# A planner that prices transfers beside weight loads differently, with its order searched anew, in an attention and MoE kernel

## The chip, the cores and the metric

The kernel runs on one NeuronCore of a Trainium2 chip. The metric is the device time of one execution in microseconds (us); lower is better. One launch computes everything.

## The reference, cut to what matters

```python
q, k, v: (4, 8, 768, 64)   proj: (64, 6)   moe_w_in: (512, 2048)   moe_w_out: (2048, 512)

q_bucket = bits of (q @ proj > 0) as one number; k_bucket the same
scores = where(q_bucket[:, None] == k_bucket[None, :], q @ k.T / 8, -1e9)
attn = exp(scores - max); attn = attn / (sum + 1e-9)
x = attn @ v                      # heads side by side: (3072, 512)
h = x @ w_in; g = s * max(h, 0)**2 + b
out = g @ w_out                   # (3072, 512)
```

All of it is in 32-bit floating point.

## The kernel before, in words

**Work.** There are 32 visits, one for each batch and head, and each has three slots of 256 queries, 96 slots in all. A slot's scores go into three banks of PSUM: six leading matmuls (L656 or L658), then a maximum over the keys on VectorE (L664), its transposes on TensorE (L675, L679) with reductions on VectorE (L677, L686), six more matmuls that add the negative maximum (L696 or L698), three exponentials on ScalarE (L703), and the products with the values (L726, later L728 and L729). The first 27 slots (9 visits) use plain float32 in their value products; the rest split each operand into two parts. For some visits the queries are split in the same way: they are loaded, transposed and split (L476 and L490 on TensorE or L493 on VectorE, then L498, L499), hashed (L514 or L527 to L532, with L540, L543, L544 behind them), and parts are copied between tiles by several DMAs that SyncE (SP) issues (L225). From the ninth visit on, q and k come in four small loads (L442) and are transposed on VectorE (L493).

**MoE.** When the eight heads of a batch have a chunk of 256 tokens ready, it goes through a DRAM tile (xd, then xc) and the two MoE matrix products follow (L814, L831). They are TensorE work that may stand anywhere between the slots' steps. None can start before the first batch's heads are done, that is before 24 slots.

**Weights.** They arrive as 32 loads of 512 KB that ScalarE (ACT) issues (L391, tile `raw`, 128 rows of 4 KB), each unpacked by two ACT instructions (L392, L393), two on VectorE (L394, L395), and more on GpSimd and ACT (L396, L398, L404). Two of them may be under way before they are unpacked (`PACE = 2`).

**Values.** From the tenth visit on, a visit's values come through one tile `vn` (L598), which ACT casts into `vs` (L603), VectorE sums (L601) and GpSimd splits (L604). ACT works strictly in its order, so what stands behind L603 waits with it; so do VectorE and SP.

**What sets the order.** All steps are added to a `Plan` with an engine, an assumed cost, a priority and, for DMAs, an assumed service time (`lag`). `Plan.order` plays a list schedule through and gives each engine one fixed order. The priority of a step is moved by `NUDGE`, a table of numbers by code line and part of the run. The plan's times are only for sorting: on the chip an instruction starts when its semaphores allow it. Two rules of the plan matter here. One assumes that TensorE slows to half speed for 3.4 us when a running figure `warm`, which falls with gaps, is under a threshold. The other is the service of DMAs; before, all shared one counter:

```python
            if lag:
                moved = max(moved, start + cost) + lag
                end = moved + LAND
```

PSUM bank 4 is shared by the small transposes, the hash matmuls (L514, L527 to L532), the sums (L578, L614) and the transposes of queries (L476, L490), one group at a time. So such a matmul right behind an L679 can't start before VectorE's L686 has read the bank.

Of the kernel before, what the change touches and what calls it, by code (L numbers as in the profile page):

```python
# [31 lines left out]
class Plan:  # L32
# [41 lines left out]
    def order(self):  # L74
# [13 lines left out]
        moved = held = late = 0.0  # L88
# [21 lines left out]
        while len(out) < n:  # L110
# [20 lines left out]
            elif e == POOL:  # L131
                cost += max(0.0, held - start)
            elif e == PE:
                part = 1 / (1 + (start - free.get(PE, 0.0)) / 6)
                warm *= part * part
                if warm < 0.48:
                    late = start + 3.4
                if start < late:
                    cost *= 2
                part = 1 / (1 + cost / 6)  # L140
                warm = 1 - (1 - warm) * (part * part)
            free[e] = start + cost
            end = start + cost + HOP[e]
            if lag:
                moved = max(moved, start + cost) + lag
                end = moved + LAND
            out.append((start, i))
# [28 lines left out]
LAND = 1.3  # L176
# [11 lines left out]
def lsh_attention_moe(ctx: ExitStack, tc, q, k, v, proj, w_in, w_out, s, b, out):  # L188
# [181 lines left out]
    def decode(u, pr):  # L370
# [20 lines left out]
        plan.add(ACT, 0.33, lambda: nc.scalar.dma_start(raw(), src.rearrange("p (n t) -> p n t", t=2)), KK("a") if u < PACE else [], rk + [("pace", u % PACE)], pr - 5, 2.2)  # L391
# [644 lines left out]
```

## Time and profile before

| | before |
|---|---|
| median of 3 runs | 985.3 us (982.86 to 987.53) |
| the profiled execution's own time | 986.14 us |
| its span, first to last instruction | 984.4 us |
| TensorE busy (PE) | 958.5 us, 97% |
| VectorE (DVE), ScalarE (ACT), GpSimd (POOL) busy | 705.9, 703.9, 681.2 us |
| mean granted TensorE clock | 0.997 |

PE is matmuls on TensorE, PEld its weight loads. Of the profiled execution's time 1.7 us lie around the span. A busy share is over the whole span: the attention of the first 24 slots, the mixed stretch and the MoE tail have different limits, so the stretches are read apart.

### The profile page before, as it was taken

The page shows a single profiled execution, that of the slowest core. Times are in us where ns is not written, and L with a number is a line of the kernel's source. Part 1 is how long each engine was busy: PE and PEld are TensorE (multiplying, and loading weights), DVE is VectorE, ACT ScalarE, POOL GpSimd, SP SyncE. Part 2 cuts the span into 40 slices and gives each one's busy share as a digit, 9 for nine tenths or more (in the row PEclk, how much of TensorE's full clock was granted, in tenths as well). Part 3 has the DMA queues.
Part 4 walks back from the last instruction along what each step waited for, and adds up shares of the span by engine and source line. Part 5 has one row for each costly group of instructions (what it writes and reads, how often), then busy time and mean ns, then how long its engine had stood idle before and what let it go on. Part 6 is the DMA issues. An engine that isn't in the chain of part 4 may idle for free.

```text
span 984.4 us, 17823 instructions
## 1 busy us (share of the span) xinstructions
PE 958.5 (97%) x6322; PEld 865.4 (88%) x6322; DVE 705.9 (72%) x1081; ACT 703.9 (72%) x1365; POOL 681.2 (69%) x641
## 2 busy tenths in 40 slices
PE   8989988999999999999999999999999999999998
PEld 7877766789999999999899999999899999989997
DVE  6897776988988898888888898888888876100000
ACT  4777766888788887879788878878787877433332
POOL 3686756779787787879697887879687878522222
PEclk9999999999999999999999999999999999999999
DMA  6583766533433443342533433442523310201000
GB/s 172 163 225 107 211 167 144 151 77 72 121 89 82 101 103 69 111 105 61 138 72 89 115 89 70 115 103 63 143 57 91 108 45 2 96 21 45 33 22 22
DMA packets 133680, 95.21 MB, mean 97 GB/s; under 512 B 101464, under 2 KB 106328, under 8 KB 133592
## 3 DMA queue, kind: packets, MB, share of 16 engines
q1 hardware_dynamic: 128248, 77.03, 31.0%
q10 hardware_dynamic: 5344, 17.05, 5.9%
q8 instruction: 50, 0.82, 0.4%
q14 instruction: 38, 0.31, 0.1%
HBM read 50.40 MB, written 18.87 MB: 70 GB/s over the span
## 4 chain that ended last, share of the span: by engine, by line
PE 88%; DVE 4%; DMA 3%; ACT 2%; issue 1%; POOL 1%; SPq 0%; DVEq 0%; ACTq 0%; POOLq 0%
PE bank L814 27%; PE bank L831 26%; PE bank L658 6%; PE bank L726 6%; PE bank L698 5%; PE bank L729 5%; PE bank L728 5%; PE bank L656 2%; DMA xc<-xd 1%; PE bank L679 1%; DVE mx L664 1%; PE bank L761 1%; PE bank L527 1%; PE bank L528 1%; DVE osb L395 1%
## 5 line engine op out<-in xcount | busy, mean ns | idle before, releaser
L814 PE MATMUL bank<-xc,w 128*128 128x256 f32 x2304 | 346.6, 284 | 2.5 <-DMA xc<-xd 2.3
L722 POOL TENSOR_TENSOR hl<-et,hl 128x512 fp32r<-128x512 f32 x207 | 267.3, 1321 | 83.6 <-ACT hl L721 78.8
L814 PEld LDWEIGHTS bank<-xc,w 128*128 128x128 f32 x2304 | 309.3, 190 | 10.5 <-DMA xc<-xd 2.8
L831 PE MATMUL bank<-w,ghb 128*128 128x512 f32 x768 | 251.7, 396 | 0.0
L822 POOL TENSOR_TENSOR glb<-rb,ghb 128x512 fp32r<-128x512 f32 x96 | 124.8, 1300 | 106.7 <-ACT ghb L821 103.8
L664 DVE TENSOR_REDUCE mx<-bank 128x256 f32<-128x1536 f32 x96 | 168.3, 1753 | 9.6 <-ACT nat L540 2.9
L703 ACT ACTIVATE et<-bank 128x512 f32<-128x512 f32 x234 | 129.1, 626 | 45.0 <-PE bank L698 30.8
L748 DVE TENSOR_REDUCE zb<-et 128x256 f32<-128x1536 f32 x69 | 120.9, 1752 | 52.3 <-ACT et L703 52.1
L831 PEld LDWEIGHTS bank<-w,ghb 128*128 128x128 f32 x768 | 136.2, 188 | 19.1
L831 PE MATMUL bank<-w,glb 128*128 128x512 f32 x384 | 152.2, 397 | 0.0
L721 ACT CAST hl<-et 128x512 fp32r<-128x512 f32 x207 | 125.4, 672 | 0.0
L819 ACT ACTIVATE rb<-bank 128x512 f32<-128x512 f32 x96 | 57.2, 596 | 93.0 <-PE bank L814 91.8
L658 PE MATMUL bank<-aq,ks 84*128 84x256 f32 x504 | 108.1, 301 | 0.2 <-ACT ex L703 0.2
L728 PE MATMUL bank<-hl,vs 128*128 128x256 f32 x414 | 107.3, 283 | 0.0
L729 PE MATMUL bank<-hl,vs 128*128 128x256 f32 x414 | 107.0, 282 | 0.0
L768 ACT ACTIVATE xpb<-bank,vmn 64x256 f32<-64x256 f32 x96 | 45.1, 470 | 66.5 <-PE bank L729 42.9
L658 PEld LDWEIGHTS bank<-aq,ks 84*128 84x128 f32 x504 | 80.1, 190 | 5.4 <-ACT ex L703 0.4
L729 PEld LDWEIGHTS bank<-hl,vs 128*128 128x128 f32 x414 | 78.5, 190 | 6.6 <-POOL hl L722 0.2
L728 PEld LDWEIGHTS bank<-hl,vs 128*128 128x128 f32 x414 | 78.0, 188 | 6.7 <-issue 0.2
L831 PEld LDWEIGHTS bank<-w,glb 128*128 128x128 f32 x384 | 72.2, 188 | 12.4 <-POOL glb L822 0.2
L839 DVE SCALAR_TENSOR_TENSOR osb<-bank,misc,bcs 128x512 f32<-128x512 f32 x22 | 16.3, 747 | 89.0 <-PE bank L831 88.7
L698 PE MATMUL bank<-bq,ks 128*128 128x256 f32 x504 | 79.4, 288 | 0.0
(144 smaller groups left out, 1581.7 us busy)
## 6 DMA issues: line engine op xcount, KB each, us to landing
xd<-xsb SPq DMA_DIRECT2D x48, 256.0 KB
xc<-xd SPq DMA_DIRECT2D x48, 256.0 KB
raw<-in_moe_w_in_dram ACTq DMA_DIRECT2D x16, 512.0 KB
raw<-in_moe_w_out_dram ACTq DMA_DIRECT2D x16, 512.0 KB
vn<-in_v_dram SPq DMA_DIRECT2D x34, 192.0 KB
out_dram<-osb SPq DMA_DIRECT2D x22, 256.0 KB
ks<-aq SPq DMA_DIRECT2D x28, 192.0 KB
ks<-bq SPq DMA_DIRECT2D x28, 192.0 KB
```

Source lines behind the costliest of these rows:

```text
L658: nc.tensor.matmul(o, ks[0:HR + NR, 0, kt], aq[0:HR + NR, cs], start=m == 0, stop=m == 1, skip_group_check=True)
L664: dve(S * TPC, lambda: nc.vector.tensor_reduce(t, sc, AX.XY, ALU.max), [("b", b) for b in pb], [tk], pr, 1.75)
L698: nc.tensor.matmul(o, ks[:, 1, kt], bq[:, cs], start=False, stop=m == 1, skip_group_check=True)
L703: act(512, lambda p=p, z=z: nc.scalar.activation(et(z) if plain(i) else pairs(z), bank[:, pb[p]] if plain(i) else bank[:, pb[p]].rearrange ...
L721: act(512, lambda z=z, y=y: nc.scalar.copy(HL[2 * y].rearrange("p (m n) -> p m n", n=CH), pairs(z)), [("e", z)], [("hl", 2 * y)], pr, 0.05)
L722: pool(512, lambda z=z, y=y: nc.gpsimd.tensor_tensor(HL[2 * y + 1].rearrange("p (m n) -> p m n", n=CH), pairs(z), f32(HL[2 * y]).rearrange ...
L728: nc.tensor.matmul(av, VS[x][:, kt], HL[2 * y][:, ms], start=(kt == 0), stop=False)
L729: nc.tensor.matmul(av, VS[x][:, kt], HL[2 * y + 1][:, ms], start=False, stop=(kt == NT - 1))
L748: dve(S * TPC, lambda: nc.vector.tensor_reduce(ZB, es, AX.XY, ALU.add), [("e", z) for z in range(NE)], ["zb"], pr, 1.75)
L814: nc.tensor.matmul(hp, wt[("wi", n, cc)][:, m % 2, fs], xc[:, m // 2, :], start=(cc == 0 and m == 0), stop=(cc == NC_ - 1 and m == 2))
L822: pool(2 * CH, lambda r=r, gh=gh, gl=gl: nc.gpsimd.tensor_tensor(gl, r, f32(gh), ALU.subtract), [rk, hk], [lk], MP)
L831: nc.tensor.matmul(bank[:, 6 + t, :], (gh, gh, gl)[n][:, ts], wt[("wo", f)][:, n % 2], start=(f == 0 and n == 0), stop=(f == NF - 1 and n ...
```

## The change: what it does

Three things change in the planner, and none in what is computed. The threshold of `warm` rises from 0.48 to 0.54. Transfers get two counters: one for SP, on which a transfer takes up to twice its service while a weight load is still being served, and one for ACT's weight loads, which SP's transfers don't delay; a weight load's assumed service rises from 2.2 to 3.0 us. And the table `NUDGE` has new numbers throughout. The loads themselves stay as they were: rows of 4 KB.

```diff
-        moved = held = late = 0.0
+        moved = loads = held = late = 0.0
...
-                if warm < 0.48:
+                if warm < 0.54:
                     late = start + 3.4
...
-            if lag:
-                moved = max(moved, start + cost) + lag
+            if lag and e == SP:
+                moved = max(moved, start + cost)
+                moved += lag + min(lag, max(0.0, loads - moved))
                 end = moved + LAND
+            elif lag:
+                loads = max(loads, start + cost) + lag
+                end = loads + LAND
...
 -        plan.add(ACT, 0.33, lambda: nc.scalar.dma_start(raw(), src.rearrange("p (n t) -> p n t", t=2)), KK("a") if u < PACE else [], rk + [("pace", u % PACE)], pr - 5, 2.2)
+        plan.add(ACT, 0.33, lambda: nc.scalar.dma_start(raw(), src.rearrange("p (n t) -> p n t", t=2)), KK("a") if u < PACE else [], rk + [("pace", u % PACE)], pr - 5, 3.0)
...
 NUDGE = {
-    0: {0: -11.9, 1: -17.1, 2: -18.8, 3: 14, 4: 4},
+    0: {0: -24.1, 1: -23.1, 2: -16.1, 3: -1.8, 4: 11.1},
...
```

In the changed file the kernel's lines stand four higher: L493 of before is L497 of the change, L603 is L607, and so on. The rows below give the order that came of it, each engine's instructions one after the other.

**First place: VectorE in slots 16 and 17**, where the first visit with small loads (tile `nat_66`) is transposed. Before, ending with L493 and the L686 behind it:

```order
L394 TENSOR_SCALAR raw_233<-osb 128x512
L686 SCALAR_TENSOR_TENSOR bq_70<-bank,ident 8x256
L395 SCALAR_TENSOR_TENSOR osb<-osb,raw_233 128x512
L775 STREAM_TRANSPOSE zpb<-zpb 128x256
L776 RECIPROCAL rc<-zpb 128x8
L664 TENSOR_REDUCE mx<-bank 128x256
L777 STREAM_TRANSPOSE zpb<-rc 128x256
L480 COPY ekb<-bank 64x384
L677 TENSOR_REDUCE nmt<-bank 128x2
L493 STREAM_TRANSPOSE nat_66<-nat_66 128x384
L686 SCALAR_TENSOR_TENSOR bq_70<-bank,ident 8x256
```

The same place in the change (L497 is the transpose):

```order
L781 STREAM_TRANSPOSE zpb<-rc 128x256
L398 TENSOR_SCALAR raw_234<-osb 128x512
L484 COPY ekb<-bank 64x384
L399 SCALAR_TENSOR_TENSOR osb<-osb,raw_234 128x512
L520 TENSOR_SCALAR eqb<-bank,misc 44x384
L668 TENSOR_REDUCE mx<-bank 128x256
L520 TENSOR_SCALAR eqb<-bank,misc 44x384
L497 STREAM_TRANSPOSE nat_66<-nat_66 128x384
L681 TENSOR_REDUCE nmt<-bank 128x2
L497 STREAM_TRANSPOSE nat_66<-nat_66 128x384
L690 SCALAR_TENSOR_TENSOR bq_71<-bank,ident 8x256
```

The transpose has moved about one slot back: it now stands in front of the L686 of slot 18 (`bq_71`) and behind both hash thresholds of `eqb`.

**Second place: the values of the tenth visit**, SP's load of `vn` and ACT's cast of it. SP before:

```order
L225 DMA ks_72<-nat_66 12x768
L225 DMA aq_68<-nat_66 12x768
L598 DMA vn<-in_v_dram 128x384
L225 DMA ks_73<-aq_69 64x768
L225 DMA ks_73<-aq_69 56x768
L225 DMA ks_73<-aq_69 8x768
L225 DMA ks_73<-bq_71 64x768
L442 DMA nat_66<-in_q_dram 32x24x32 x2
```

SP in the change:

```order
L229 DMA ks_72<-nat_66 12x768
L229 DMA aq_68<-nat_66 12x768
L229 DMA ks_73<-bq_71 64x768
L446 DMA nat_66<-in_q_dram 32x24x32 x2
L446 DMA nat_66<-in_k_dram 32x24x32 x2
L602 DMA vn<-in_v_dram 128x384 x2
```

The load of `vn` has moved behind the four loads of `nat_66`. ACT before, from the second L540 of `nat_66` (the step that leads to SP's copies above) to the cast L603:

```order
L540 COPY nat_66<-bank 24x384
L703 ACTIVATE ex_86<-bank 128x512
L703 ACTIVATE ex_87<-bank 128x512
L398 CAST w_1416<-osb 128x512
L498 ACTIVATE aq_69<-nat_67,misc 128x384
L557 ACTIVATE vmn<-bank 64x1
L498 ACTIVATE aq_69<-nat_67,misc 128x384
L391 DMA raw_239<-in_moe_w_in_dram 128x1024
L392 ACTIVATE osb<-raw_238 128x512
L393 ACTIVATE raw_237<-raw_237 128x512
L768 ACTIVATE xpb<-bank,vmn 64x256
L603 CAST vs_1447<-vn 128x6x64
```

ACT in the change, from the pair of weight loads on (seven more instructions stand between the L544 of `nat_66`, which is L540 of before, and this pair):

```order
L395 DMA raw_239<-in_moe_w_in_dram 128x1024
L395 DMA raw_1110<-in_moe_w_in_dram 128x1024
L707 ACTIVATE et<-bank 128x512 x3
L770 ACTIVATE zpb<-bank 64x256
L561 ACTIVATE vmn<-bank 64x1
L772 ACTIVATE xpb<-bank,vmn 64x256
L402 CAST w_1474<-osb 128x512
L396 ACTIVATE osb<-raw_239 128x512
L397 ACTIVATE raw_239<-raw_239 128x512
L402 CAST w_1503<-osb 128x512
```

The cast (L607) follows after three further exponentials, an L770, an L544 and an L772: eight exponentials stand between the L540 and the cast where two stood. Two weight loads are now issued one after the other here.

**Third place: TensorE in slot 5**, where the hash of a visit (L530 to L532) meets the transposes. Before:

```order
L675 MATMUL bank<-ident,mx 128x128 x2
L726 MATMUL bank<-ex_84,evb 128x256
L658 MATMUL bank<-aq_68,ks_72 128x256 x4
L679 MATMUL bank<-ident,nmt 8x128
L530 MATMUL bank<-aq_69,pjs 24x384
```

In the change:

```order
L679 MATMUL bank<-ident,mx 128x128 x2
L730 MATMUL bank<-ex_83,evb 128x256
L730 MATMUL bank<-ex_84,evb 128x256
L683 MATMUL bank<-ident,nmt 8x128
L730 MATMUL bank<-ex_84,evb 128x256
L662 MATMUL bank<-aq_68,ks_72 128x256 x4
L534 MATMUL bank<-aq_69,pjs 24x384
```

A value product and four leading matmuls have moved from in front of the small transpose (L679 of before, L683 of the change) to behind it, between it and the hash that waits for bank 4.

## Rows read from the trace of the kernel before

**Rows 1.** The page's first line: the span.
```profile
span 984.4 us, 17823 instructions
```

**Rows 2.** Windows: stretch (us), its length, each engine's busy time, clock, DMA share, GB/s.
```profile
0.00:200.00 200.00, 180.79 (x991) 149.70 (x992) 155.79 (x259) 140.21 (x277) 128.07 (x133) 0.98 0.64 167
120.00:140.00 20.00, 16.49 (x87) 13.46 (x86) 14.07 (x24) 14.04 (x29) 10.21 (x11) 0.91 0.67 172
160.00:180.00 20.00, 15.97 (x80) 13.14 (x79) 13.49 (x23) 11.53 (x25) 10.03 (x9) 0.91 0.70 170
200.00:845.00 645.00, 642.13 (x4483) 594.17 (x4482) 543.33 (x811) 519.06 (x1015) 520.62 (x483) 1.00 0.35 89
```

**Rows 3.** Timeline of TensorE: start, us, instructions, [idle before, and who ended it].
```profile
126.75 1.13 PE L726 MATMUL bank<-ex,vs 128*128 128x256 f32 x4 [0.81 <-ACT ex L703]
...
132.64 0.55 PE L476 MATMUL bank<-ident,nat 128*128 128x128 f32 x3 [1.98 <-DVE bq L686]
...
134.34 1.94 PE L726 MATMUL bank<-ex,vs 128*128 128x256 f32 x4 [0.45 <-ACT ex L703]
```

**Rows 4.** Timeline of VectorE at the first stall.
```profile
131.71 0.58 DVE L493 STREAM_TRANSPOSE nat<-nat 128x384 f32<-128x384 f32 x1 [1.62 <-DMA nat<-in_k_dram]
```

**Rows 5.** The chain that ended last, in order of time: start, us, what.
```profile
124.17 2.69 DMA aq<-nat
...
126.93 0.69 SPq L442
...
129.06 2.62 DMA nat<-in_k_dram
...
158.81 5.06 DMA vn<-in_v_dram
```

**Rows 6.** Timeline of ACT at the second stall.
```profile
163.90 0.51 ACT L603 CAST vs<-vn 128x384 fp32r<-128x384 f32 x1 [3.17 <-DMA vn<-in_v_dram]
```

**Rows 7.** Timeline of TensorE at the second stall.
```profile
165.49 2.07 PE L726 MATMUL bank<-et,evb 128*128 128x256 f32 x4 [2.73 <-ACT et L703]
```

**Rows 8.** Groups of DVE: line, engine, op, tiles, shapes, count | busy, mean ns | idle.
```profile
L394 DVE TENSOR_SCALAR raw<-osb 128x512 int32<-128x512 int32 x32 | 18.5, 578 | 0.0
L516 DVE TENSOR_SCALAR eqb<-bank,misc 44x384 f32<-44x384 f32 x4 | 2.7, 670 | 2.5 <-PE bank L514 2.4
L480 DVE COPY ekb<-bank 64x384 f32<-64x384 f32 x4 | 2.2, 557 | 0.3 <-ACT eqb L479 0.2
```

**Rows 9.** The same view, groups of ACT.
```profile
L703 ACT ACTIVATE et<-bank 128x512 f32<-128x512 f32 x234 | 129.1, 626 | 45.0 <-PE bank L698 30.8 <-issue 7.2 <-PE bank L696 3.3
L768 ACT ACTIVATE xpb<-bank,vmn 64x256 f32<-64x256 f32 x96 | 45.1, 470 | 66.5 <-PE bank L729 42.9 <-PE bank L726 22.7
L498 ACT ACTIVATE aq<-nat,misc 128x384 fp32r<-128x384 f32 x48 | 29.9, 623 | 1.9 <-DVE nat L493 1.4
L540 ACT COPY nat<-bank 24x384 f32<-24x384 f32 x48 | 22.6, 472 | 1.2
L393 ACT ACTIVATE raw<-raw 128x512 int32<-128x512 uint32 x32 | 21.7, 679 | 0.2
L392 ACT ACTIVATE osb<-raw 128x512 f32<-128x512 f32 x32 | 21.7, 678 | 3.5 <-POOL w L404 2.1 <-DMA raw<-in_moe_w_in_dram 1.1
L398 ACT CAST w<-osb 128x512 fp32r<-128x512 f32 x32 | 19.8, 623 | 3.1 <-POOL osb L396 2.9
L766 ACT ACTIVATE zpb<-bank 64x256 f32<-64x256 f32 x27 | 10.3, 381 | 2.4 <-PE bank L726 2.1
```

**Rows 10.** Timeline of TensorE: a matmul of bank 4 right behind an L679.
```profile
112.39 0.55 PE L490 MATMUL bank<-ident,nat 128*128 128x128 f32 x3 [0.51 <-DVE zhl L686]
```

**Rows 11.** Waits of the whole span: engine, what waited <- for whom: us, times, longest.
```profile
ACT osb L392 <- DMA raw<-in_moe_w_in_dram: 1.1, 1, 1.1
```

**Rows 12.** Timeline of ACT at a pair of weight loads, and the unpacking of the first.
```profile
93.40 0.33 ACTq L391 DMA_DIRECT2D raw<-in_moe_w_out_dram  x1
93.77 0.45 ACTq L391 DMA_DIRECT2D raw<-in_moe_w_in_dram  x1
...
98.20 0.67 ACT L392 ACTIVATE osb<-raw 128x512 f32<-128x512 f32 x1
```

More of the change, by code (lines that the diff above doesn't have):

```diff
@@ L390, in decode @@
         plan.add(None, 0.0, new, [], rk + held, pr - 5)
-        plan.add(ACT, 0.33, lambda: nc.scalar.dma_start(raw(), src.rearrange("p (n t) -> p n t", t=2)), KK("a") if u < PACE else [], rk + [("pace", u % PACE)], pr - 5, 2.2)
+        plan.add(ACT, 0.33, lambda: nc.scalar.dma_start(raw(), src.rearrange("p (n t) -> p n t", t=2)), KK("a") if u < PACE else [], rk + [("pace", u % PACE)], pr - 5, 3.0)
         act(512, lambda: nc.scalar.activation(g, raw()[:, :, 1].bitcast(F32), AF.Copy, scale=float(2.0**-112)), rk + [("pace", u % PACE)], [gk], pr, 0.06)
```

180 rows, old and new, of the table NUDGE are left out of this document.

## The prediction

> **What bounds the kernel now.** I read the page first, then windows by stage, then TensorE's timeline and the chain that ended last where the windows showed a loss. The span is 984.4 us [rows 1], and the change adds or removes no matmul, so the time moves only by TensorE's idle time and by its clock. The windows tell where there is something to win. From 200 to 845 us TensorE is busy 642.1 of 645 us: 2.9 us idle in all, at the full clock; behind 845 it does MoE work alone. From 0 to 200 us it is busy 180.8, so 19.2 us are idle, and the mean clock is 0.98 [rows 2]. In that stretch there is no MoE work to fill with, as the first batch isn't done. The planner changes the order everywhere, but only the first 200 us have much to give or lose.
>
> Two windows of that stretch stand out, 120 to 140 and 160 to 180 us: 3.5 and 4.0 us idle, and a clock of 0.91 in both [rows 2]. Each holds one long wait, and both begin with a DMA.
>
> The first: TensorE waits 1.98 us for VectorE's L686 before an L476 [rows 3]. VectorE was late because L493 stands in front of that L686 in its order, and had waited 1.62 us for the load of k [rows 4]. The chain shows that load as the last of a series on SP: a copy of aq landing 2.69 us after its issue, then one load issue after the other at about 0.69 us, then 2.62 us for the last to land [rows 5].
>
> The second: TensorE waits 2.73 us for an exponential [rows 7]. ACT was late because the cast L603 stood in front of the exponentials and waited 3.17 us for vn [rows 6], which took 5.06 us from issue to landing [rows 5].
>
> After each the clock is low: four L726 take 1.94 and 2.07 us [rows 3, 7], where four take 1.13 at the full clock [rows 3].
>
> **The change, part by part.** The planner's assumed times sort and nothing else, so its three edits are priced by the order that came of them.
>
> *Term 1, the transpose L493: -2.0 us.* Between the last L544 of the tile and the first L493, VectorE's order has 12 rows before and 16 in the change. Net of what both have, the change puts in front of the transpose two L516 (0.67 each), an L480 (0.56) and an L394 (0.58) [rows 8], an L777 coming in for an L677 of about the same length: 1.34 + 0.56 + 0.58 = 2.5 us more work. SP's order from the copies to these loads is the same. 2.5 is more than the 1.62 waited [rows 4], so the wait closes with some 0.9 us to spare, and TensorE's 1.98 us [rows 3] go. The bounds are 0 (the load is late by as much again) and 1.98. I take all of it. What is late next there is L686 behind the second L493, which then waits for VectorE's own work.
>
> *Term 2, the cast L603: -2.7 us.* SP now issues vn behind the four loads of nat_66, which first wait for the copy of aq to land (2.69 us), and which take 4 x 0.69 us to issue [rows 5]. Before, vn stood directly behind that copy's issue, about 0.7 us. So vn is issued 2.69 + 2.76 - 0.7 = 4.8 us later. ACT's cast has moved too: between the L540 and the cast there are now six more exponentials (0.626 each), three more L766 (0.381), two more L392 and two L393 (0.678, 0.679), one more each of L768, L398 and L540 (0.470, 0.623, 0.472), and two L498 fewer (0.623) [rows 9]. That is 3.76 + 1.14 + 1.36 + 1.36 + 0.47 + 0.62 + 0.47 - 1.25 = 7.9 us of work, 3.1 more than the 4.8, against a wait of 3.17 [rows 6]. By work alone the wait would just close. But ACT is busy only 11.5 of 20 us there [rows 2], since it waits for TensorE between its steps, so 7.9 us of work take up to 13.7 us, and the cast should find vn landed. TensorE's 2.73 us [rows 7] go. The bounds are again 0 and the whole. Where vn is late all the same, three exponentials no longer stand right behind it, but the next three do.
>
> *Term 3, the clock: -3.0 us.* Each of the two windows lost 0.09 x 20 = 1.8 us of clock [rows 2]; at half speed four L726 lost 0.81 and 0.94 us. With the waits in front of them gone the clock has no reason to fall there. Some of the slow work lay beside waits that remain (0.45 us before the four at 134.34 [rows 3]), so I take 1.5 of 1.8 for each; bounds 0 and 3.6. The raised threshold itself is priced at nothing: it only makes the planner shun gaps.
>
> *Term 4, matmuls of bank 4 right behind an L679: -1.0 us.* They wait for L686; one shows 0.51 us idle [rows 10]. The order has such bare pairs, with an L696 or a bank-4 matmul directly behind, in ten of the first 24 slots before and in eight of the change: slot 5, shown above, is one that got a cover. 2 x 0.5. Bounds 0 and, if all covers that got shorter or longer count, about 2.
>
> *Term 5, new waits: +2.8 us.* A new order has waits that the old one had not, and the trace of before can't show them. The lower bound is 0; the upper one is all that the two stalls of before cost, 2.0 + 2.7 + 3.6 = 8.3. The nearest row is one stall like that of [rows 7] without a fall of the clock, 2.7; the planner's model of the DMAs is still rough, and the first 200 us have many consumers of copies.
>
> The weight loads are not changed themselves. Their longer assumed service and the new table put them at other places; ACT has waited for one only once, 1.1 us [rows 11]. I price that at nothing while the exponentials behind L392 cover it; what it costs if not is rival B.
>
> The Trainium skill, page "DMA: Bandwidth & Descriptors", section "Issuing engines are not separate DMA queues", says that DMAs from ScalarE and SyncE run on the same 16 engines and interleave. By that the new rule is half right: SP's copies are drawn out beside a load, but the load is drawn out too, which the plan now leaves out. The trace agrees as far as it goes: vn, issued beside a weight load, took 5.06 us and the load of k 2.62 [rows 5], though vn is twice the size. By the row of waits the sum stays as it is; by the page's rule it would be that of rival B.
>
> **The sum.** -2.0 - 2.7 - 3.0 - 1.0 + 2.8 = -5.9 us. The profiled execution took 986.1 us, so its like would take 980.2; the median of the runs shown is 985.3, 0.8 lower, so I forecast 985.3 - 5.9 = 979.4 us, 0.6% less. The three runs of before spread over 4.7 us, so about 0.5% (4.9 us) is what can be told from no change.
>
> **The rivals.**
>
> *A, the waits only move.* The table was searched on a model that did not foresee the two stalls; the wait for k was not beside a weight load at all by its chain [rows 5], so the new rule doesn't even price it. Then about as many new stalls arise, with their clock: term 5 at 8.3 instead of 2.8, sum -0.4, 984.9 us. For it: both orders are equally full of copies with little cover. Against: the two consumers that I could count have got their room.
>
> *B, slower: weight loads late on ACT.* The mechanism is that of [rows 6] with `raw` in place of vn: L392 waits for its load, and the exponentials behind it wait too. The place is the pair of loads issued together around the tenth visit's values: from the first of them to its L392 the change has three exponentials, L766, L768 and L398, 1.88 + 0.38 + 0.47 + 0.62 = 3.4 us of work [rows 9], where before the same tile had about 6.7. One such stall costs 2.7 of wait and 1.5 of clock, 4.2 us. Terms 1 to 4 give 8.7, so four stalls are needed: -8.7 + 16.8 = +8.1, 993.4 us; at three it is within 0.5%. Against: before, the first load of a pair was unpacked 4.8 us after its issue without a wait [rows 12], so 3.4 us of work plus ACT's waits for TensorE can be late by 1.4 at most.
>
> *C, better.* If term 5 is 0, term 3 is 3.6 and a quarter of the 14.5 us left idle in the first 200 us (19.2 less 1.98 and 2.73) goes as well, the sum is -2.0 - 2.7 - 3.6 - 1.0 - 3.6 = -12.9, 972.4 us. For it: values of slots 19 to 22 now stand one slot later in TensorE's order, which gives the exponentials more room just where most was lost. Against: 14.5 us spread over many short waits that no rule of the change addresses.
>
> **How the numbers follow.** My forecast has 0.55, A 0.25, B 0.12, C 0.08. The forecast's own range is 974 to 983 (term 5 from 0 to 5, term 3 from 2 to 3.6); about a fifth of it lies above 980.4 and so within 0.5%. Faster: 0.45 + 0.08 + 0.03 of A = 0.56. Same: 0.10 + 0.13 of A + 0.01 of B = 0.24. Slower: 0.09 of A + 0.11 of B = 0.20. The range reaches to 972 for C and to 990 for what A holds beyond its middle; half of C and most of B, with a little of A, are left out.
>
> **What would show it.** Term 1: no wait of VectorE's L497 for a DMA, and no TensorE idle over 1 us before an L480 (the L476 of before). Term 2: no wait of ACT's L607 for vn over 1 us. Term 3: all 20 us windows of the first 200 us at a clock of 1.00. Term 4: one or two waits fewer of bank-4 matmuls for L690. Term 5: TensorE's idle time from 0 to 200 us should be near 19.2 - 2.0 - 2.7 - 1.0 + 2.8 = 16.3 us, and the stretch after 200 us unchanged within 2 us. The prediction is wrong if a new wait of over 2 us with a low clock behind it stands in that stretch, whether for a copy (A) or for `raw` at L396 (B), or if the mixed stretch has lost fill.

## The result, and the profile after

The change is slower. Its median is 995.2 us over 5 runs (992.82 to 995.69); 5 runs of before beside it took 987.51 (982.86 to 988.08). The ratio is 1.008, with a 95% interval of 1.0055 to 1.0106. The forecast was 979.4.

The page's first lines of the change's profiled execution, which took 992.82 us: the span, and each engine's busy time.

```profile
span 991.0 us, 17864 instructions
...
PE 961.1 (97%) x6322; PEld 867.6 (88%) x6322; DVE 705.2 (71%) x1081; ACT 701.8 (71%) x1365; POOL 680.6 (69%) x641
```

Against the span of before [rows 1] that is 6.6 us more: TensorE is idle 29.9 us (991.0 less 961.1) where it was 25.9 (984.4 less 958.5), and it is busy 2.6 us longer for the same number of matmuls. Slow clock doesn't explain that part: the mean granted clock is 0.997 in both profiled executions, and I found no other cause. The windows, with columns as in [rows 2]:

```profile
0.00:200.00 200.00, 177.51 (x960) 146.27 (x960) 152.42 (x257) 136.25 (x271) 123.88 (x128) 0.98 0.62 162
60.00:80.00 20.00, 16.92 (x88) 13.35 (x87) 16.02 (x24) 16.41 (x33) 13.13 (x14) 0.93 0.72 192
100.00:120.00 20.00, 17.60 (x90) 14.76 (x89) 12.49 (x23) 10.90 (x22) 13.48 (x15) 0.91 0.48 123
120.00:140.00 20.00, 15.91 (x91) 12.83 (x89) 13.65 (x22) 13.46 (x27) 9.83 (x10) 1.00 0.53 150
160.00:180.00 20.00, 19.11 (x99) 15.46 (x97) 16.09 (x21) 14.37 (x29) 11.84 (x9) 1.00 0.60 135
200.00:845.00 645.00, 641.36 (x4470) 593.65 (x4469) 545.19 (x810) 518.37 (x1018) 519.36 (x483) 1.00 0.35 89
```

The stretch behind 200 us is what it was (641.4 busy, 642.1 before). The first 200 us are idle 22.5 us instead of 19.2. The windows at 120 and 160 us have their full clock back; those at 60 and 100 us have lost it. So the first stall of before is gone, part of the second has come back at another reader of `vn` (the third below), and others have come. The timelines show three of them (columns as in [rows 3]). The first, on ACT and then on TensorE:

```profile
112.12 0.40 ACT L783 CAST xsb<-xpb 128x256 fp32r<-128x256 f32 x1 [2.80 <-DMA xd<-xsb]
```

```profile
113.67 1.13 PE L730 MATMUL bank<-ex,eva 128*128 128x256 f32 x4 [2.37 <-ACT ex L707]
...
114.98 1.91 PE L730 MATMUL bank<-ex,eva 128*128 128x256 f32 x4
```

ACT's cast into `xsb` waits for the copy of the old `xsb` to DRAM, the exponentials stand behind the cast, and TensorE's value products wait for these. The next four L730 take 1.91 us: the clock has fallen (from 116 to 118 us the granted clock is 0.50, the lower of its two levels, 1.2 instead of 2.4 GHz). The chain that ended last has that copy, and a second one:

```profile
107.20 4.83 DMA xd<-xsb
...
134.63 4.13 DMA aq<-nat
```

ACT had issued a weight load 2.3 us ahead of the first and 0.6 us ahead of the second:

```profile
104.91 0.34 ACTq L395 DMA_DIRECT2D raw<-in_moe_w_in_dram  x1
...
134.01 0.33 ACTq L395 DMA_DIRECT2D raw<-in_moe_w_out_dram  x1
```

For the second copy, TensorE waits itself, at the leading matmuls of the next visit; no fall of the clock follows here:

```profile
138.90 0.95 PE L662 MATMUL bank<-aq,ks 84*128 84x256 f32 x6 [2.12 <-DMA aq<-nat]
```

The third is on VectorE: the sum of the tenth visit's values (L605) waits for `vn`, with L547 and L548 behind it, and TensorE waits 1.73 us for that L548, again with no fall of the clock behind it. The cast L607 waits 1.12 us for the same `vn`, which took 3.60 us:

```profile
179.88 0.82 DVE L605 TENSOR_REDUCE pj<-vn 128x64 f32<-128x384 f32 x1 [1.13 <-DMA vn<-in_v_dram]
```

```profile
182.04 0.44 PE L679 MATMUL bank<-ident,mx 128*128 128x128 f32 x2 [1.73 <-DVE nat L548]
```

No weight load was beside this `vn`, but a pair of them stood one step ahead. The four loads of `nat` in front of `vn` on SP waited until the copies `ks` and `aq` had landed, and these were issued right behind two weight loads (at 164.39 and 165.04 us):

```profile
165.04 0.33 ACTq L395 DMA_DIRECT2D raw<-in_moe_w_in_dram  x1
```

```profile
166.44 0.71 SPq L229 DMA_DIRECT2D aq<-nat  x1
...
173.35 1.40 SPq L446 DMA_DIRECT2D nat<-in_q_dram  x2
```

SP's wait, from the view of waits of 155 to 182 us:

```profile
SPq L446 <- DMA ks<-nat: 5.3, 1, 5.3
```

No experiment moved this pair, so its part in the third stall is argued and not shown.

The fourth place has no long wait. Between 67 and 77 us TensorE waits 0.5 to 0.6 us five times, the last three of them as below, and then its clock falls all the same: the last four L730 take 2.08 us.

```profile
74.68 0.27 PE L683 MATMUL bank<-ident,nmt 128*8 128x128 f32 x1 [0.60 <-DVE nmt L681]
75.55 0.25 PE L582 MATMUL bank<-misc,vn 128*64 128x1 f32 x2 [0.60 <-DVE bq L690]
...
77.20 2.08 PE L730 MATMUL bank<-ex,vs 128*128 128x256 f32 x4 [0.50 <-ACT ex L707]
```

One more thing stands in the runs themselves, each of which lists its mean granted clock: the median is 0.994 in the 5 runs of the change, and 0.9975 in the 22 runs of before that stand beside the first experiments. So the profiled execution of the change (0.997) is a mild one. By spans of 993 and 985 us the means come to 6.0 and 2.5 us, a difference of 3.5. Runs at the same clock give less: at 0.994, 0.996 and 0.997 the change took 995.2, 994.1 and 992.8 us, where the runs of before beside the experiments have medians of 988.1, 989.5 and 986.8. So 5 to 7 us of the loss of 8 stand at equal clock, and 1 to 3 are clock.

My theory: a copy that SP issues just behind a weight load lands 2 us later than it does alone, the new order put other consumers of copies in the way of TensorE's feeders, and the clock can fall behind such waits. Rivals: the copies are late by themselves, whatever the loads do; the stretch is elastic, so that no single wait costs what it shows; or the new rules, or the new table, are bad in themselves.

### The profile page after: what moved, and what is told of

Its sections match the earlier page's. It is cut to its first block, busy times and chain, and to the rows that moved or that the text cites. A ratio compares the mean times of both kernels' runs of the same rounds, so it can differ in the third digit from the quotient of the medians.

```text
span 991.0 us, 17864 instructions
## 1 busy us (share of the span) xinstructions
PE 961.1 (97%) x6322; PEld 867.6 (88%) x6322; DVE 705.2 (71%) x1081; ACT 701.8 (71%) x1365; POOL 680.6 (69%) x641
## 4 chain that ended last, share of the span: by engine, by line
PE 88%; DMA 4%; DVE 3%; ACT 2%; POOL 2%; issue 1%; SPq 0%; DVEq 0%; ACTq 0%; POOLq 0%
PE bank L818 26%; PE bank L835 26%; PE bank L662 6%; PE bank L730 6%; PE bank L702 5%; PE bank L732 5%; PE bank L733 5%; PE bank L660 2%; DMA xc<-xd 1%; PE bank L683 1%; DMA xd<-xsb 1%; PE bank L765 1%; PE bank L531 1%; PE bank L532 1%; DMA vn<-in_v_dram 1%
## 5 line engine op out<-in xcount | busy, mean ns | idle before, releaser
L772 ACT ACTIVATE xpb<-bank,vmn 64x256 f32<-64x256 f32 x96 | 44.9, 468 | 50.8 <-PE bank L733 37.4
L843 DVE SCALAR_TENSOR_TENSOR osb<-bank,misc,bcs 128x512 f32<-128x512 f32 x22 | 16.3, 749 | 90.0 <-PE bank L835 89.7
```

## The experiments

All but four kernels keep a table and its rules and only move single steps of the finished order. This function does it; a list names each step by its line and its count in the order, and the step goes behind another one with what depends on it.

```diff
     queue = plan.order()
+    queue = later(plan, queue)
...
+def later(plan, queue):
+    made = {}
+    for i in queue:
+        made.setdefault(plan.steps[i][2].__code__.co_firstlineno, []).append(i)
+    for (a, m), (b, n) in LATER:
+        j, k = made[a][m], made[b][n]
+        p, q = queue.index(j), queue.index(k)
...
+        go = {j}
+        for i in queue[p:q + 1]:
+            if plan.steps[i][5] & go:
+                go.add(i)
...
+        queue[p:q + 1] = [i for i in seg if i not in go] + [i for i in seg if i in go]
```

Ratios are to the runs of before beside each kernel, whose median was 986.0 to 986.2 us (987.5 for the change).

| kernel | us, median | ratio to before, 95% interval | median clock of its runs |
|---|---|---|---|
| change | 995.2 | 1.008 (1.0055 to 1.0106) | 0.994 |
| 1 before, room for two consumers | 980.6 | 0.9942 (0.992 to 0.9965) | 1.000 |
| 2 change, room for two consumers | 991.5 | 1.0055 (1.0034 to 1.0077) | 0.9945 |
| 3 change, two weight loads later | 989.4 | 1.0033 (1.0013 to 1.0053) | 0.996 |
| 4 new rules, old table | 1008.7 | 1.0231 (1.0205 to 1.0257) | 0.994 |
| 5 old rules, new table | 1018.9 | 1.0337 (1.0305 to 1.0368) | 0.988 |
| 6 = 2 and 3 together | 989.3 | 1.0032 (1.0016 to 1.0049) | 0.998 |
| 7 change, short waits covered | 998.6 | 1.0126 (1.01 to 1.0151) | 0.993 |
| 8 = 1 and eight covers | 980.7 | 0.9942 (0.9922 to 0.9963) | 1.000 |
| 9 threshold only, old table | 1003.1 | 1.0167 (1.0146 to 1.0187) | 0.991 |
| 10 counters only, old table | 1013.9 | 1.0297 (1.0271 to 1.0322) | 0.9905 |
| 11 = 6 and two repairs more | 989.4 | 1.003 (1.0016 to 1.0044) | 0.998 |
| 12 = 1 and one consumer more | 982.4 | 0.9958 (0.9941 to 0.9974) | 0.997 |

### 1. Before, with terms 1 and 2 alone

```diff
+LATER = [
+    ((498, 8), (703, 53)),
+    ((493, 0), (480, 7)),
+    ((493, 1), (480, 7)),
+    ((603, 0), (703, 65)),
+]
```

> The kernel before, its table and rules kept, with only the three consumers moved that terms 1 and 2 speak of: both L493 of nat_66 behind the L480 that follows, the L498 that they feed behind a later exponential, and the cast L603 of vn behind three exponentials. SP's and TensorE's orders stay. If the two stalls are priced rightly (terms 1 to 3: 2.0 + 2.7 and up to 3.0 of clock), it takes 4.7 to 7.7 us less than before, about 978 to 982 us, no window of 120 to 180 us below a clock of 1.00, and the change lost its time only by new stalls. If a stall that goes is made good by the next wait (the rival that the stretch is elastic), it takes less than 2 us less, and the idle time from 0 to 200 us stays near 19.

It takes 980.6 us, 5.4 less than before (0.58%). The windows of 120 and 160 us:

```profile
120.00:140.00 20.00, 16.92 (x99) 13.62 (x99) 16.66 (x27) 15.61 (x33) 10.29 (x12) 1.00 0.67 165
160.00:180.00 20.00, 18.00 (x98) 14.86 (x96) 18.69 (x29) 15.44 (x33) 13.68 (x12) 1.00 0.79 186
```

Both have the full clock, the cast of `vn` finds it landed, and so does the L493 for `k`. The mean clock is 1.000 in most of its runs. So the stalls of [rows 4, 6] were real and cost about what the prediction said (terms 1 to 3 make 4.7 to 7.7). The sum is made up otherwise, though: TensorE's idle time from 0 to 200 us fell from 19.2 to 16.4 us, 2.8 of the 4.7 that the two waits took, and the clock gave about 2.5 (0.0025 of the span). The rival of an elastic stretch, which put it at under 2 us with some 19 us idle, falls here. What cost the change its time lies in what else it moved.

### 2 and 3. The change: consumers later, or weight loads later

Experiment 2 moves the late consumers, 3 moves the loads beside the late copies and no consumer. (The L605 that the first expectation puts in the eleventh visit is the tenth's.)

```diff
+LATER = [
+    ((783, 5), (707, 41)),
+    ((605, 0), (548, 10)),
+]
```

```diff
+LATER = [
+    ((395, 18), (707, 41)),
+    ((395, 22), (707, 53)),
+]
```

> The change with two consumers moved that its trace shows late: the cast L783 (it waited 2.8 us for a copy xd to land, TensorE 2.37 behind it, then a low clock, 1.7) behind three exponentials, and the L605 of the eleventh visit's values behind the L547 and L548 that wait behind it (TensorE 1.73 there and 0.89 after). If single consumers standing in front of TensorE's feeders cost the time, 4 to 6.5 us go, 989 to 991 us against 995. If the rival holds, that the new order lost fill everywhere and the stalls are where it shows by chance, less than 2 us go.

> The change with every consumer left in place and two weight loads issued later instead: the one issued 2.3 us ahead of the copy xd at 107 us goes behind three exponentials and more of ACT's work, and so does the one issued 0.6 us ahead of the copy aq at 134.6 us. If a copy is late because a weight load is under way beside it, xd lands after 2.5 to 3.3 us instead of 4.83, aq after 2.4 to 3 instead of 4.13, TensorE's waits of 2.37 and 2.12 fall to about 0.6 each with the low clock behind the first gone: about 5 us less than the change, 990 us. If the copies are late for another reason (their own pattern, SP's queue), both land as late as before and the time stays within 1 us of 995. If the loads are then late themselves, ACT waits for raw at L396, 1 to 3 us.

Experiment 3 settles the mechanism for the first two stalls. Its SP issues the same copies in the same order; only the loads are gone from beside them. The copy `xd`, then the cast that waited 2.80 us for it, with no wait now:

```profile
107.38 0.50 SPq L229 DMA_DIRECT2D xd<-xsb  x1
```

```profile
109.66 0.41 ACT L783 CAST xsb<-xpb 128x256 fp32r<-128x256 f32 x1
```

From issue to the cast it is 2.28 us, so the copy landed in at most that, instead of 4.83. The copy `aq` is issued at 131.30, and TensorE needs it at:

```profile
131.30 0.75 SPq L229 DMA_DIRECT2D aq<-nat  x1
```

```profile
133.79 0.95 PE L662 MATMUL bank<-aq,ks 84*128 84x256 f32 x6 [0.39 <-DMA aq<-nat]
```

2.49 us after the issue at most, instead of 4.13; the wait of 2.12 us is 0.39. ACT now issues the weight loads nearest to them at 99.64 and 111.58 us for `xd`, and at 126.64 and 136.66 for `aq`. So a weight load beside them made these copies at least 1.6 and 2.6 us later, and the rival that they are late by themselves falls. The time is 989.4 us, 0.47% less than the change, 4.6 us, as expected. The third stall of the change, TensorE's wait for L548, is left with 1.8 us at 177 us.

Experiment 2 gave less than expected, 0.25% or 2.5 us, though TensorE's wait at the first stall fell from 2.37 to 0.45 and the window 100 to 120 us got its clock back: in the profiled execution, two other windows lost theirs.

```profile
80.00:100.00 20.00, 18.76 (x95) 15.10 (x94) 12.47 (x19) 11.92 (x25) 12.91 (x13) 0.90 0.55 154
...
140.00:160.00 20.00, 18.39 (x85) 14.84 (x85) 16.16 (x26) 14.04 (x29) 13.32 (x15) 0.86 0.61 141
```

Its ten runs have clocks from 0.991 to 1.000 and times from 989.2 to 997.0 us. What a removed wait returns in clock differs from one execution to the next.

### 4, 5, 9 and 10. Rules and table apart

Experiment 4 is the change with the table of before, 5 is before with the new table. 9 is before with the threshold alone, 10 is 4 without the threshold:

```diff
-                if warm < 0.48:
+                if warm < 0.54:
```

```diff
-                if warm < 0.54:
+                if warm < 0.48:
```

> The three edits of the planner with the table of before, so that rules and table are told apart; it computes all the same. If the rules themselves set the loss, the time is near that of the change, 993 to 997 us. If they are harmless and the new table set it, it is within 3 us of before, 983 to 989. My theory is that any new order has stalls of its own until it is measured: a table that wasn't searched under its rules gives a worse order than either, 995 to 1010 us, with new places of idle time over 1 us in the first 200 us, and some in the mixed stretch.

> The other half of the split: the planner's rules and service of before with the new table. With the rules alone at 1009 us, the theory that a table only fits the rules under which it was searched expects this order to be worse than both kernels as well, 995 to 1010 us. If the new rules are what costs (rival), it comes out at or under 986 us; if the new table is what is bad under any rules, about 1015 us or more.

> The kernel before with one edit of the planner alone: the threshold of warm at 0.54 instead of 0.48, table of before. The three edits together, with the table of before, gave 1008.7 us. If the threshold is nearly nothing, as the prediction priced it, the order changes little: within 3 us of 986. If any edit of a rule makes an unsearched order, this one gives 995 to 1010 us as well, with new stalls in the first 200 us at other places than the second kernel of this call.

> The other edits alone: two counters for the transfers and the service of 3.0 us for a weight load, threshold 0.48, table of before. If these carry the loss of the rules with the old table, about 1009 us with the 4.9 us wait of L607 for vn, as with all three edits; if the loss is that of any unsearched order, 995 to 1010 at other places. If they bring what they are for, fewer and shorter waits of ACT and VectorE for copies, under 986 us.

All four are worse than both kernels: 1008.7, 1018.9, 1003.1 and 1013.9 us. 4 and 9 fall in the range expected of an order that wasn't searched; 10 lies above it. 5 is so late that by its expectation the table would be bad under any rules; but under the new rules the same table gives 995.2. 10 has another longest wait than I named. Each table was far better under the rules it came with, even where one threshold differs; so these runs can't tell whether a rule is good. They do show where each kernel has its waits. Summed over the rows of the view of waits from 20 to 200 us for TensorE, VectorE and ACT that wait for a DMA: with the single counter 6.3 us (before), 6.9 (5) and 8.1 (9); with the two counters 10.2 (change), 13.2 (10) and 16.0 (4). But 3.1 of the change's 10.2 and 0.7 of kernel 10's are waits for weight loads; for SP's transfers alone the change has 7.1, less than kernel 9. Two such rows of 10, and of 4:

```profile
ACT xsb L783 <- DMA xd<-xsb: 3.9, 3, 2.9
...
DVE nat L497 <- DMA nat<-in_q_dram: 6.6, 1, 6.6
```

```profile
ACT xsb L783 <- DMA xd<-xsb: 6.8, 3, 3.1
...
ACT vs L607 <- DMA vn<-in_v_dram: 4.9, 1, 4.9
```

With the two counters and the old table consumers stand closer to their copies than these allow; for the change itself the sums show no clear difference. A reason may lie in the rule: it adds at most the copy's own service, which the plan takes as 0.16 us for the 36 KB of `aq<-nat` (36,864 / 250,000 + 0.01), while experiment 3 found 1.6 us or more; the old counter put such a copy behind the whole 2.2 us of the load. That this is why the waits grew is argued, not shown, since each table also has its own order.

### 6 and 11. The change, repaired further

6 has the edits of 2 and 3. 11 adds these, the first four as in experiment 7, the last for ACT's L396, which waited 2.38 us for its load at 34.5 us:

```diff
+    ((656, 25), (683, 7)),
+    ((656, 26), (683, 7)),
+    ((656, 28), (683, 8)),
+    ((656, 29), (683, 8)),
+    ((396, 4), (707, 8)),
```

> The two edits on the change together: both weight loads later, the cast L783 and the L605 later. Alone they gave 3.7 and 5.8 us, and the trace of the loads-only kernel still showed the wait of 1.8 us for L548 behind L605 and one weight load needed late (2.1 at L396). If they add where they touch different stalls, the L605 move brings about 1.8 us more than the loads alone, 986 to 988 us, with 17 to 18 us idle from 0 to 200 us. If the stretch is elastic, it stays at 989 or above.

> The change with the edits of the sixth kernel (989.3 us) and two more: the four L662 of slots 6 and 7 behind the L683 as in the seventh, but VectorE's order left alone, since its L402 was late there only because L398 and L399 had moved; and ACT's L396 that waits up to 2.4 us for its load near 34 us behind the three exponentials that follow. If what the change lost is the sum of such single waits and of the clock behind them, 0.5 to 2 us go near 36 us, 1 near 67 and 75, and the fall of the clock at 77 (1.7) may go: 985 to 987 us, level with before. If what remains is lost otherwise, 989 as before.

Both miss: 989.3 and 989.4 us, what experiment 3 has alone (the 3.7 and 5.8 us in the first expectation compare medians; by ratios they are 2.5 and 4.6). The single waits did go. In 6 no wait of TensorE in the first 200 us is over 1.2 us, and its median clock is 0.998, level with before. But its runs stay 0.3% above before, and the profiled execution is the fastest of the 12, 985.6 us against 988.1 to 994.0 for the others, so the trace doesn't show what the typical run loses. The covers of 11 moved the waits in front of L683, as in 8 below, and the clock still falls at 78 us; and behind 200 us its profiled execution waits more for `xc` than that of 6, which has 1.0 us of it:

```profile
PE bank L818 <- DMA xc<-xd: 4.1, 6, 1.3
```

That is 3.1 us of the 4.3 by which these two executions differ, at the same mean clock of 0.998. So the waits for `xc` in the mixed stretch change by some 3 us from one execution to the next, or with the edits; one profile of each can't tell. In the first 200 us the rival of the elastic stretch fits what is left: long waits could be removed, the many short ones moved.

### 7, 8 and 12. Short waits

7 covers three short waits of the change in slots 6 to 8. 8 adds to kernel 1 what term 4 spoke of, at eight places; 12 adds one late cast to it.

```diff
+    ((656, 25), (683, 7)),
+    ((656, 26), (683, 7)),
+    ((656, 28), (683, 8)),
+    ((656, 29), (683, 8)),
+    ((398, 10), (688, 8)),
```

```diff
+    ((652, 19), (679, 5)),
+    ((652, 20), (679, 5)),
...
+    ((652, 74), (679, 23)),
```

```diff
+    ((779, 2), (703, 23)),
```

> The change with three short waits covered in slots 6 to 8 and nothing else: the four L662 in front of the L683 at 66.4 us and those at 73.4 us go behind it, ahead of the L480 and the L582 that wait for bank 4, and VectorE's L398 and L399 in front of the L681 at 74.2 us go behind the L690. By term 4's price three waits of 0.5 to 0.6 us go, 1.6 us; if the fall of the clock at 77.2 us came of this row of short waits, its 1.7 us go as well, 3.3 together, 992 us. If the covers only delay VectorE's L668 of the next slot (rival), nothing is won, and the window 60 to 80 us keeps its clock of 0.93.

> The kernel before with the room of the first experiment and, besides, term 4 at scale: at eight places in the first 24 slots up to four L658 that stood in front of an L679 now stand behind it, so that the bank-4 matmul or the L696 that follows has cover. At 0.5 us each that is 4 us under the 980.6 of the first experiment, 976 to 977 us, and the idle time from 0 to 200 us falls from 16.4 to about 12.5. If the L658 behind L679 make VectorE's next L664 late by as much, nothing is won: 980 to 981 us, with longer waits of L675 or of L726 in place of those of L476, L490, L514 and L530.

> The kernel before with the room of the first experiment and one consumer more: the cast L779 that waits 1.36 us for a copy xd at 67 us, with TensorE's longest remaining wait (1.40) behind it, goes behind three exponentials. If a wait of TensorE that has one late consumer as its cause goes whole, 1.2 to 1.4 us under the 980.6 of the first experiment: 979.3 us, and no wait of L726 over 0.8 us near 68 us. If it only comes back at the next copy of xd, 980.6.

7 is slower than the change, 1.0126 against 1.008. The L480 and the L582 no longer wait, but VectorE's L398 and L399, which I put back to free the L681, feed GpSimd's unpacking, whose L402 on ACT stands in front of the exponentials:

```profile
80.39 0.62 ACT L402 CAST w<-osb 128x512 fp32r<-128x512 f32 x1 [1.37 <-POOL osb L400]
```

```profile
81.69 2.07 PE L730 MATMUL bank<-ex,vs 128*128 128x256 f32 x4 [2.56 <-ACT ex L707]
```

The waits of 0.51 and 0.60 in front of the L480 and the L582 went, the one in front of the L683 stayed at 0.52, and the 0.50 in front of the L730 became 2.56 with the clock behind it. Part of the loss isn't from the edit: a wait of 1.86 us at 38.7 us and a window of 40 to 60 us at 0.92 lie ahead of it.

8 gains nothing over kernel 1, 980.7 against 980.6. In the view of waits of kernel 1 and then of 8, TensorE waits less for L686 and more for the L677 in front of it:

```profile
PE bank L679 <- DVE nmt L677: 2.0, 3, 0.9
PE bank L514 <- DVE bq L686: 1.8, 3, 0.6
PE bank L476 <- DVE bq L686: 1.4, 3, 0.6
```

```profile
PE bank L679 <- DVE nmt L677: 3.6, 6, 1.3
...
PE bank L514 <- DVE bq L686: 1.0, 3, 0.6
PE bank L476 <- DVE bq L686: 0.6, 1, 0.6
```

A cover behind L679 is taken from in front of it: L679 is asked for earlier, and VectorE isn't earlier. TensorE's idle time from 0 to 200 us did fall, from 16.4 to 15.3 us where 12.5 was expected, but the runs are no faster.

12 is no better than 1 (its interval overlaps that of 1 and lies a little above). The wait of 1.40 us is gone, but GpSimd waits for the same cast, and its share of the next values stands behind it:

```profile
69.73 0.73 POOL L780 TENSOR_TENSOR xsb<-xpb,xsb 128x256 fp32r<-128x256 f32 x1 [3.10 <-ACT xsb L779]
...
72.25 0.85 POOL L576 TENSOR_TENSOR vn<-vn 128x64 f32<-128x64 f32 x1
```

TensorE's L578 now waits 1.23 us for that L576. Besides, the median clock of its runs is 0.997 against 1.000.

## Why the prediction was wrong, point by point

**Term 1 was right.** No L497 waits for a DMA, and the largest wait before an L480 is 0.51 us. In kernel 1, too, the two waits went, though only 2.8 of the 4.7 us of terms 1 and 2 came back as idle time.

**Term 2 was half right.** The cast waits 1.12 us instead of 3.17, just over the mark of 1 us, and no exponential is late behind it. The delay of `vn` was mis-sized: it was taken as issued 5.45 us behind the issue of the copy of aq (2.69 + 2.76) and was issued 9.75 behind it (176.19 - 166.44), because the copies in front of it landed late. And `vn` has a second reader, the sum L605 on VectorE, whose place I hadn't looked at: it stands in front of L547 and L548, and 1.73 of the 2.73 us came back through it. That the waits themselves cost what terms 1 to 3 say is shown by experiment 1, which moved the consumers alone and got 5.4 us.

**Term 3, the clock, was a wrong step.** It read "with the waits in front of them gone the clock has no reason to fall there", and it was right there, but it was booked as if no other place could lose clock. The converse fails as well: TensorE waited 2.12 and 1.73 us in the change without a fall behind. The two windows at 0.91 became windows at 0.93, 0.98 and 0.91: in the profiled execution nothing was won instead of 3.0 us, and over the runs the change loses 1 to 3 us more to the clock than before.

**Term 4 came true by its sign and brought no time that can be shown.** TensorE's waits of bank-4 matmuls for L686 were ten before, one of them the stall of Term 1, and are eight for L690 in the change. But eight covers added in experiment 8 changed no time, so the price of 0.5 us for each is not borne out.

**Term 5 is the step that failed most, and with it the weight loads, which were priced at nothing.** It was put at 2.8 us, one stall without a fall of the clock. TensorE's idle time from 0 to 200 us should have been 16.3 us; it is 22.5. From 19.2 less the 4.7 that went, new waits brought 8.0 us: 2.37, 2.12 and 1.73 at the places shown, 0.89 just ahead of the third (an L730 at 178.75 us that waits for an L772), and 0.9 net in short ones. That alone is nearly the upper bound of 8.3, which was meant to hold the clock as well. The moved weight loads were looked at only as loads that may come late themselves; that they make SP's copies late was left out, and by experiment 3 two of them cost 4.6 us. The price of a new order's stalls was read from one row of a wait without its clock; the same trace had two such stalls with a fall of the clock each in an order that had been searched, and that was the better measure for the new one. (The lower end of the forecast's own range is mis-added, too: with term 5 at 0 and term 3 at 3.6 the terms give -9.3, so 976 and not 974.)

**The rivals.** A named the right mechanism, waits that only move, and its place, copies with little cover; at 984.9 us it was too small, since it left the clock at its gain of 3.0. With the idle time as measured (8.0 - 4.7 = 3.3 us) and the 1 to 3 us of clock, it would have come to 4 to 6 of the 7.7 us by which the medians differ. B's place was wrong: L396 did wait up to 2.4 us for a load, at 34 us, but in the change's profile TensorE waited only 0.51 us behind it; in the kernels 2, 6 and 7 it waited 0.95 to 1.86 us there. At the pair that B named, L396 didn't wait for its load; the copies issued right behind that pair are those of the third stall. The rule of the Trainium skill that the prediction weighed, page "DMA: Bandwidth & Descriptors", section "Issuing engines are not separate DMA queues", says that SP's copies and ACT's loads run on the same engines and interleave. Experiment 3 agrees in that a load beside them makes the copies late, by at least 1.6 and 2.6 us; whether they are drawn out or stand behind the load, no run here shows.

**What stays open.** With its three stalls out of the way the change is still 0.3% behind before, and 0.9% behind before without its two. The windows show no single place for it, and the kernels 11 and 12 show that short waits come back elsewhere. I did not settle what carries it: short waits in the first 200 us, or the waits for `xc` behind them, which were 1.0 us in the profiled execution of 6 and 4.1 in that of 11. Open too are the 2.6 us by which TensorE is busy longer in the change's profile, and whether the new rules by themselves are good.

**The best version** is kernel 1, the kernel before with four steps moved: 980.6 us, 0.58% faster than before and 1.4% faster than the change.

## What to carry to other kernels

An order that is searched on a model has stalls where the model is wrong, and a change of the model moves them; price the new ones by what the old order shows, with the clock as a range, and don't book the removed ones alone. Ask of a moved transfer not only whether it is late itself, but which copies it now stands beside. Two long waits of which the trace names the late transfer and the one instruction in the way are worth moving by hand: four steps gave 5.4 us where the new rules and search lost 8, though two such moves on the change gave only 2.5. A short wait is another matter: before covering one, ask what the cover stood in front of, and who waits for what moves back.

## What the runs showed of the hardware

A copy of 36 KB landed 4.13 us after its issue when a weight load of 512 KB had been issued 0.6 us earlier, and within 2.49 when the nearest one ahead had been issued 4.7 us earlier; the copy `xd` took 4.83 with a load issued 2.3 us earlier, and at most 2.28 with that load moved behind it.

Waits of TensorE don't settle whether its clock falls. It fell behind a row of five waits of 0.5 to 0.6 us within 10 us (at 77.20 us in the change, where the granted clock is 0.50 from 78 to 80 us, and behind much the same row in the kernels 2, 3 and 6; in 11 behind three waits of 0.56, 1.08 and 0.52). It did not fall behind a single wait of 1.40 us in kernel 1, nor behind the 2.12 us at 138.90 in the change, where it stays at 1.00 to 160 us; in kernel 2 it fell behind the same wait, there 2.28 us long. The kernels 1 and 12 have the same matmuls and almost the same waits from 173 to 176 us (0.90, 0.50 and 0.26 us in kernel 1, 0.98, 0.51 and 0.25 in 12), and only in 12 does the clock fall:

```profile
175.96 1.13 PE L726 MATMUL bank<-ex,evb 128*128 128x256 f32 x4 [0.26 <-ACT ex L703]
```

```profile
175.42 1.92 PE L726 MATMUL bank<-ex,evb 128*128 128x256 f32 x4 [0.25 <-ACT ex L703]
```

So a wait has no fixed price in clock. The Trainium skill, page "TensorE: Matmul & The Clock Gate", section "A second HAM failure mode: psum-queue depth-cycling", tells of a kernel whose short, frequent idle times between groups of matmuls make the clock go up and down; the row at 77.20 agrees with that, the row of kernel 1 does not.

Executions of one kernel differ in how often the clock falls: kernel 2 ran at mean clocks from 0.991 to 1.000, in 996.0 and 990.6 us, while most runs of kernel 1 stood at 1.000, and all within 3.8 us of each other.
